# Mixing tiles moved between output products and routing steps, and a split moved from GpSimd to the Vector engine, in a fused attention, gMLP and mixture-of-experts kernel

## The chip, the cores and the metric

The kernel runs on one core of a Trainium2 chip. The core has a Tensor engine (PE, matrix products, with a separate queue for loading weights), a Vector engine (DVE), a Scalar engine (ACT), GpSimd (POOL), and SyncE (SP), which issues most of the DMAs. Each takes its instructions in order and waits for the others by semaphores. The metric is the device time of one execution in microseconds, as a median of several runs.

## What is computed

Three layers follow each other on two batches of 768 tokens with 384 features (8 heads of 48).

```
# 1 linear attention, per batch and head
state = alpha[t] * state + outer(k[t], v[t]);  y[t] = q[t] @ state
# 2 gMLP: d_ff = 1024, u and v have 512 columns each
h = gelu(x @ w_in);  u, v = split(h)
v_n = (v - mean(v)) / sqrt(var(v) + 1e-6) * g_ln
v_s = w_sg @ v_n + b_sg            # mixes the 768 tokens
x = x + (u * v_s) @ w_out
# 3 eight experts, one per token
fresh = argmax(x @ w_gate)         # e = fresh, or the token before's e when its local gate is >= 0.5
p = softmax(x @ w_gate)
out = p[e] * (relu(x @ w1[e]) @ w2[e])
```

## The kernel before, in words

**Products in three passes.** A float32 operand is split into a high part (`hi`, by ACT, L161) and a low part (`lo`, the difference, L162, by DVE or GpSimd as `pick` says), and `mm3` (L378) multiplies hi by hi, hi by lo and lo by hi. So one "term" is three products on PE.

**Stages.** Attention fills the first half. Then the second part of the gMLP and the routing run for each batch in two parts of tokens: 384 and 384 in batch 0, 512 and 256 in batch 1. From about 257 us to the end the eight experts run.

**The order of the middle** is a tuple, `SEQ`, which is worked through entry by entry. An entry has a letter, a batch and a part:

- `s`: `gmlp_s`, one mixing tile of 128 of the 512 columns. Eighteen products into `pvs`, then on DVE the bias and gain (L494), the factor u (L496), and the split into `g` (L161 on ACT, L162 on DVE). A part has four such tiles.
- `o`: `gmlp_out`, 36 products `po` from the four `g` and `w_out`, then three additions `x += po` on DVE (L512).
- `r`: one step of `route`. The first step multiplies x with the gate weights and the identity (`pr`, L527), takes logits (L530) and the maximum, and on DVE makes a chain of small operations (L545 to L559) that ends in `kf`. The second step turns `kf` round on PE (`pkr`, `pfr`, L564) and scans along the tokens (`er`, L571). The third counts the tokens of each expert (`pe`: L588, L589, L595, L597; `rsel` L600, `cl` L603). The fourth makes one-hot tiles `L` and `R` (L615, L616), multiplies them (`pid`, L618) and adds them to the slot table `tab` (L623). A further `r` of a finished part does nothing.
- `h1`: a step of batch 1's hidden layer. `l1`, `w0`, `k1`: loading the weights of expert 0, splitting them (`we_e_lo`), and loading two weights of expert 1.
- `e0`: `early` (L625). It reads the first slots of `tab` (`egid`), starts two gathers of token rows with GpSimd (`xs_first`, L726), and then calls `banks(5)`: the pool of eight PSUM banks is closed, and one of five, with three banks `px` beside it, is opened. Tiles that are written later in the program lie in the new pool.

The last part's route (batch 1, part 1) has more: its 256 rows are split into `xe` (L162, by the engine that `XEE` names), multiplied into `px` with the first rows (`px` L650 from `xs_first`, L661 from `xe`), and split to `xhl_e`, the first expert's input. Then the expert products begin (`ph_e` into `hhl_e` L756 and L757, then `pmy_e`).

**Who sets the order on an engine.** The program is written in SEQ's order. A tile scheduler then sets each engine's instruction order, looking a short way ahead, so that products of one step stand between those of another. Across the change of the PSUM pool it does not.

Of the kernel before, what the change touches and what calls it, by code (L numbers as in the profile page):

```python
# [38 lines left out]

HSEQ0 = 'vvuvuuvvuuuvuu'  # L40
HSEQ1 = 'vvvuvvvuuuuuuu'
SEQ = ('s00', 's00', 's00', 's00', 'x1', 's01', 's01', 's01', 'o00', 'r00', 's01', 'h1', 'r00', 'h1', 'r00', 'o01', 'h1', 'r00', 'r01', 'r00', 'h1', 'h1', 'r01', 'h1', 'r01', 'h1', 'h1', 'r01', 'h1', 'h1', 'h1', 'h1', 'r01', 'h1', 'h1', 's10', 's10', 's10', 's10', 'l1', 'w0', 's11', 'o10', 'w0', 's11', 'r10', 'r10', 's11', 'r10', 's11', 'r10', 'k1', 'k1', 'o11', 'r10', 'e0', 'r11', 'r11', 'r11', 'r11', 'r11')
INIT = ('u', 'u', 'u', 'w0', 'u', 'u', 'u', 'w1', 'w2')
ULOAD = (2, 3, 4, 5, 6, 7, 8, 7, 9, 9)
WIN = (4, 7, 6, 10, 13, 13)
# [18 lines left out]
SG = (3,) * 16  # L64
XS_E = (1,) * 12
NS_E = (1,) * 12
XEE = 0
NUNIT = 21

KEEP_T = -1.5 * 2.0 ** -23  # L70
# [2 lines left out]
class Layer:  # L73
# [441 lines left out]
    def route(self, b, hf, xT):  # L515
# [7 lines left out]
        for i in range(T):  # L523
# [11 lines left out]
            if end:  # L535
                xe = rw.tile([P, 2, DM], F32R, tag="xe", name=f"xe_{i}", bufs=T)
                self.split(xe[:, 0], xe[:, 1], xt, self.pick(XEE >> i))
                parts.append(xe)
# [288 lines left out]
    def run(self):  # L827
# [12 lines left out]
        with ExitStack() as c1:  # L840
# [84 lines left out]
            def step(nm):  # L925
                c, b, hf = nm[0], int(nm[1]), int(nm[2:3] or 0)
                if c == "s":
                    gs[b, hf].append(self.gmlp_s(b, hf, len(gs[b, hf]), vh[b], uh[b]))
                elif c == "o":
                    self.gmlp_out(b, hf, xT[b], gs[b, hf])  # L930
                    routes[b, hf] = self.route(b, hf, xT[b])
                elif c == "r":
                    next(routes[b, hf], None)
                elif c == "x":
                    xhl.append(self.x_split(1, xT[1]))
                    nonlocal_hidden.append(self.gmlp_h(1, xhl[1], vh[1], uh[1], HSEQ1))
                elif c == "h":
                    next(nonlocal_hidden[0])
                elif c == "e":
                    self.early()  # L940
                elif c == "k":
                    ahead.extend(self.expert_load(1, "e1", which=(len(ahead),)))
                elif c == "l":
                    raw.extend(self.expert_load(0, "e0"))
                elif c == "w":
                    ws[0].append(self.expert_split(raw.pop(0)))

            nonlocal_hidden, ahead = [], []
            for nm in SEQ:
                step(nm)  # L950
# [77 lines left out]
```

## Time and profile before

| what | us |
|---|---|
| median of 3 timed runs | 410.6 (410.39 to 410.85) |
| device time of the profiled execution | 409.02 |
| its span | 407.3 |
| PE busy | 380.8 (94% of the span) |
| DVE busy | 304.0 (75%) |
| ACT busy | 201.9 (50%) |
| POOL busy | 94.0 (23%) |

The profiled execution is one run, 1.6 us below the median of the timed ones, and has 1.7 us outside of its span. In the page, "busy" is time with an instruction of the engine under way, and a row of the timeline begins with the start in us from the span's start, then the time of the row, engine, line and operation, the output and inputs, the count, and in brackets the idle time before it and what ended it. Products on PE overlap in their rows: the distance of two starts is what one costs.

### The profile page before, as it was taken

How to read it: one execution, taken by the hardware profiler on the slowest of the kernel's cores; microseconds unless marked ns; L12 is line 12 of the kernel's file. 1: busy time of each engine (PE TensorE's matmuls, PEld its weight loads, DVE VectorE, ACT ScalarE, POOL GpSimd, SP SyncE). 2: the span in 40 equal slices, each digit the busy share in tenths (PEclk: the TensorE clock that was granted, in tenths of full speed). 3: DMA queues.
4: the chain of work that ended last, by engine and by line, in shares of the span. 5: the costliest groups of instructions: out<-in, count | busy, mean ns of one | idle time of the engine just before them, and what ended most of it. 6: DMA issues, size and time to landing. Idle time of an engine off the chain costs nothing. (4 is left out here: it accounts for less than half of the span.)

```text
span 407.3 us, 7658 instructions
## 1 busy us (share of the span) xinstructions
PE 380.8 (94%) x2798; PEld 328.1 (81%) x2798; DVE 304.0 (75%) x721; ACT 201.9 (50%) x465; POOL 94.0 (23%) x114
## 2 busy tenths in 40 slices
PE   8995997999999997999999896999899999999992
PEld 3663555678777996898988794899899999999991
DVE  7999999274777799866967876979886685994220
ACT  2534545465594644436562422758475563943110
POOL 1533753332240321000000004515222141300101
PEclk9997998599999999999999999999999999999998
DMA  8988877001123210110150263999756749200000
GB/s 219 300 214 209 228 217 211 22 23 36 59 53 110 92 39 2 59 38 23 33 202 2 77 228 89 362 310 354 268 174 224 259 135 330 65 0 33 32 2 26
DMA packets 34743, 54.56 MB, mean 134 GB/s; under 512 B 6243, under 2 KB 24957, under 8 KB 34704
## 3 DMA queue, kind: packets, MB, share of 16 engines
q1 hardware_dynamic: 32528, 48.08, 37.8%
q0 software_dynamic: 2176, 5.98, 4.7%
q8 instruction: 23, 0.38, 0.4%
q14 instruction: 16, 0.13, 0.1%
HBM read 46.91 MB, written 5.55 MB: 129 GB/s over the span
## 5 line engine op out<-in xcount | busy, mean ns | idle before, releaser
L378 PE MATMUL ph_e<-xhl_e,we_e_hi 128*128 128x256 f32 x384 | 69.2, 282 | 0.1
L162 DVE TENSOR_TENSOR we_e_lo<-wr_e,we_e_hi 128x384 fp32r<-128x384 f32 (+1 forms) x112 | 61.5, 608 | 9.3 <-ACT we_e_hi L161 4.8
L378 PE MATMUL pmy_e<-we_e_hi,hhl_e 128*128 128x384 f32 x256 | 67.0, 338 | 1.6 <-DVE hhl_e L757 1.6
L161 ACT ACTIVATE we_e_hi<-wr_e 128x384 fp32r<-128x384 f32 (+1 forms) x112 | 55.2, 564 | 26.6 <-PE pmy_e L378 17.8
L378 PEld LDWEIGHTS ph_e<-xhl_e,we_e_hi 128*128 128x128 f32 x384 | 59.4, 188 | 0.6 <-DVE xhl_e L162 0.6
L378 PE MATMUL ph_e<-xhl_e,we_e_lo 128*128 128x256 f32 x192 | 53.8, 281 | 0.0
L378 PEld LDWEIGHTS pmy_e<-we_e_hi,hhl_e 128*128 128x128 f32 x256 | 46.3, 188 | 1.8 <-DVE hhl_e L757 1.8
L378 PE MATMUL pmy_e<-we_e_lo,hhl_e 128*128 128x384 f32 x128 | 42.8, 336 | 0.0
L771 POOL DMA_INDIRECT out_dram<-my_e,sid x16 | 16.5, 1032 | 101.1 <-DVE my_e L770 87.5
L756 ACT ACTIVATE hhl_e<-ph_e 128x256 fp32r<-128x256 f32 x64 | 23.1, 382 | 32.7 <-PE ph_e L378 32.2
L232 POOL TENSOR_SCALAR_AFFINE_SELECT at<-at 128x384 f32<-128x384 f32 x32 | 29.1, 931 | 38.8 <-ACT at L230 38.7
L378 PEld LDWEIGHTS ph_e<-xhl_e,we_e_lo 128*128 128x128 f32 x192 | 36.7, 191 | 0.0
L757 DVE SCALAR_TENSOR_TENSOR hhl_e<-ph_e,hhl_e 128x256 fp32r<-128x256 f32 x64 | 24.2, 416 | 12.1 <-ACT hhl_e L756 12.1
L378 PE MATMUL pvs<-sg_lo,v_hi 128*128 128x384 f32 (+2 forms) x96 | 32.3, 337 | 0.0
L378 PE MATMUL pvs<-sg_hi,v_hi 128*128 128x384 f32 (+2 forms) x96 | 32.2, 340 | 0.0
L378 PE MATMUL pvs<-sg_hi,v_lo 128*128 128x384 f32 (+2 forms) x96 | 31.3, 336 | 0.0
L378 PE MATMUL pv<-wv_hi,xhl 128*128 128x512 f32 x72 | 26.6, 430 | 0.0
L378 PE MATMUL pu<-xhl,wu_hi 128*128 128x384 f32 x96 | 25.6, 344 | 0.0
L378 PE MATMUL po<-g,wo_hi 128*128 128x384 f32 (+2 forms) x96 | 25.0, 342 | 0.1
L378 PEld LDWEIGHTS pmy_e<-we_e_lo,hhl_e 128*128 128x128 f32 x128 | 24.1, 188 | 0.0
L770 DVE TENSOR_SCALAR my_e<-pmy_e,xs_e 128x384 f32<-128x384 f32 x16 | 9.8, 615 | 18.5 <-PE pmy_e L378 18.4
L280 PE MATMUL py<-at,io 128*64 128x128 f32 (+1 forms) x192 | 21.0, 294 | 2.0 <-ACT at L230 2.0
(196 smaller groups left out, 793.9 us busy)
## 6 DMA issues: line engine op xcount, KB each, us to landing
wr_e<-in_moe_w_dram SPq DMA_DIRECT2D x32, 768.0 KB, 7.3
io<-in_alpha_dram SPq DMA_DIRECT2D x16, 169.8 KB, 5.5
io<-in_k_dram SPq DMA_DIRECT2D x16, 168.0 KB, 5.6
io<-in_q_dram SPq DMA_DIRECT2D x16, 168.0 KB, 5.1
io<-in_v_dram SPq DMA_DIRECT2D x16, 144.0 KB, 4.7
sraw<-in_moe_w_sg_dram SPq DMA_DIRECT2D x3, 768.0 KB, 4.7
x2d<-xt SPq DMA_DIRECT2D x12, 192.0 KB, 2.0
x<-y SPq DMA_DIRECT2D x24, 72.0 KB, 2.5
```

The source lines that it names most:

```text
L161: return (self.nc.scalar.activation(out=hi, in_=src, func=AF.Copy), eng.tensor_tensor(out=lo, in0=src, in1=hi.bitcast(F32), op=ALU.subtract))
L162: eng.tensor_tensor(out=lo, in0=src, in1=hi.bitcast(F32), op=ALU.subtract))
L232: nc.gpsimd.affine_select(out=at[:, j], in_=at[:, j], compare_op=ALU.is_ge, fill=0.0, base=0, pattern=[[0, NCH], [1, P]], channel_multipli ...
L280: nc.tensor.matmul(py[64 * j:64 * j + m, cs], g["v"][:, o:o + m], at[:, j, c, :], start=True, stop=not inter)
L378: self.nc.tensor.matmul(out, l[a], r[c], start=start and i == 0 and p == 0, stop=stop and i == n - 1 and p == 2)
L756: nc.scalar.activation(out=hh, in_=ph, func=AF.Relu)
L757: nc.vector.scalar_tensor_tensor(out=hl, in0=ph, scalar=0.0, in1=hh.bitcast(F32), op0=ALU.max, op1=ALU.subtract)
L770: nc.vector.tensor_scalar(out=y, in0=py, scalar1=prob[i], scalar2=None, op0=ALU.mult)
L771: nc.gpsimd.indirect_dma_start(out=self.out2, out_offset=bass.IndirectOffsetOnAxis(ap=sid[:, i:i + 1], axis=0), in_=y, in_offset=None, bou ...
```

## The change

Two constants change. In SEQ, batch 0 has one mixing tile of part 1 between `o00` and the first `r00` instead of ahead of `o00`. In batch 1, `o10` comes ahead of all four tiles of part 1, and the tiles stand between its routing steps; the fifth, empty, `r10` goes; and `e0` now stands ahead of `k1`, `k1` and `o11`. `XEE` goes from 0 to 3: for the last two tiles of 128 rows the low part `xe` is made by DVE and not by GpSimd.

```diff
-SEQ = (... 'x1', 's01', 's01', 's01', 'o00', 'r00', 's01', 'h1', ...
-       's10', 's10', 's10', 's10', 'l1', 'w0', 's11', 'o10', 'w0', 's11', 'r10', 'r10', 's11', 'r10', 's11', 'r10',
-       'k1', 'k1', 'o11', 'r10', 'e0', 'r11', ...)
+SEQ = (... 'x1', 's01', 's01', 'o00', 's01', 'r00', 's01', 'h1', ...
+       's10', 's10', 's10', 's10', 'l1', 'w0', 'o10', 'w0', 's11', 'r10', 's11', 'r10', 's11', 'r10', 's11', 'r10',
+       'e0', 'k1', 'k1', 'o11', 'r11', ...)
-XEE = 0
+XEE = 3
```

What it does to the instruction order is shown at three places of batch 1. In these rows the first number of a name is the batch; of `pvs` and `vs` the second is the tile of columns and the third the part, of `po` the second is the row block and the third the part, of `pe`, `pr` and `kf` the second is the part.

On PE, at the first part's output products, before:

```order
L378 MATMUL pvs_1_0_1_2507<-sg2_hi_1552,v1_3_hi_2145 128x256
L378 MATMUL pvs_1_0_1_2507<-sg2_lo_1553,v1_3_hi_2145 128x256
L378 MATMUL pvs_1_0_1_2507<-sg2_hi_1552,v1_3_lo_2146 128x256
L378 MATMUL po_1_0_0_2532<-g_1_0_0_2410,wo_hi_1562 128x512
L378 MATMUL po_1_1_0_2533<-g_1_0_0_2410,wo_hi_1562 128x512
L378 MATMUL po_1_2_0_2534<-g_1_0_0_2410,wo_hi_1562 128x512
L378 MATMUL pvs_1_1_1_2582<-sg0_hi_1378,v1_0_hi_1909 128x256
L378 MATMUL pvs_1_1_1_2582<-sg0_lo_1379,v1_0_hi_1909 128x256
```

The same place after:

```order
L378 MATMUL pvs_1_0_0_2391<-sg2_hi_1552,v1_3_lo_2146 128x512
L378 MATMUL pvs_1_1_0_2416<-sg2_hi_1552,v1_3_lo_2146 128x512
L378 MATMUL pvs_1_2_0_2441<-sg2_hi_1552,v1_3_lo_2146 128x512
L378 MATMUL pvs_1_3_0_2466<-sg2_lo_1553,v1_3_hi_2145 128x512
L378 MATMUL pvs_1_3_0_2466<-sg2_hi_1552,v1_3_lo_2146 128x512
L378 MATMUL po_1_0_0_2507<-g_1_0_0_2410,wo_hi_1562 128x512
L378 MATMUL po_1_1_0_2508<-g_1_0_0_2410,wo_hi_1562 128x512
L378 MATMUL po_1_2_0_2509<-g_1_0_0_2410,wo_hi_1562 128x512
L378 MATMUL pvs_1_0_1_2557<-sg0_hi_1378,v1_0_hi_1909 128x256
```

The first tile of part 1 (`pvs_1_0_1`), whose products stood ahead of the first `po`, now follows the first three of them, and the end of the first tile of part 0 (`pvs_1_0_0`) stands five products ahead of `po`. The second tile of part 1 (`pvs_1_1_1`) goes from there to the middle of the twelve `pr`, 15 of its products behind the first four and three behind the last.

On DVE, in the chain from the logits of batch 1's first part to `kf`, before:

```order
L547 TENSOR_SCALAR kf_1_0_2639<-lg_1_0_2606 128x4
L552 TENSOR_TENSOR d_1_0_2647<-lg_1_0_2606,m_1_0_2641 128x32
L549 MEMSET nk_1_0_2640 1x1
L550 MEMSET kf_1_0_2639 1x1
L555 TENSOR_TENSOR ik_1_0_2649<-iotam_1239,nk_1_0_2640 128x32
L557 SCALAR_TENSOR_TENSOR ca_1_0_2651<-d_1_0_2647,ik_1_0_2649 128x32
L559 TENSOR_REDUCE kf_1_0_2639<-ca_1_0_2651 128x4
```

The same chain after:

```order
L547 TENSOR_SCALAR kf_1_0_2615<-lg_1_0_2582 128x4
L494 SCALAR_TENSOR_TENSOR vs_1_1_1_2649<-pvs_1_1_1_2630,gln_1253,bsg_1256 128x256
L552 TENSOR_TENSOR d_1_0_2623<-lg_1_0_2582,m_1_0_2617 128x32
L549 MEMSET nk_1_0_2616 1x1
L550 MEMSET kf_1_0_2615 1x1
L496 TENSOR_TENSOR vs_1_1_1_2649<-vs_1_1_1_2649,u_1_0_2129 128x256
L555 TENSOR_TENSOR ik_1_0_2625<-iotam_1239,nk_1_0_2616 128x32
L578 TENSOR_REDUCE sm_1_0_2670<-ex_1_0_2668 128x4
L557 SCALAR_TENSOR_TENSOR ca_1_0_2627<-d_1_0_2623,ik_1_0_2625 128x32
L579 TENSOR_SCALAR sm_1_0_2670<-sm_1_0_2670 128x4
L559 TENSOR_REDUCE kf_1_0_2615<-ca_1_0_2627 128x4
```

The two DVE operations of the tile that moved (L494 and L496 of `vs_1_1_1`) and two small softmax sums now stand inside of the chain.

On PE, from the counting of batch 1's first part to its slot table, before:

```order
L597 MATMUL pe_1_0_2701<-oh_1_0_2707,onesb_1229 128x8
L378 MATMUL po_1_0_1_2766<-g_1_1_0_2526,wo_hi_1562 128x256
L378 MATMUL po_1_0_1_2766<-g_1_1_0_2526,wo_lo_1563 128x256
...
L378 MATMUL po_1_2_1_2768<-g_1_1_2_2695,wo_hi_1562 128x256
L618 LDWEIGHTS L_1_0_2721
L618 MATMUL pe_1_0_2701<-R_1_0_2722,L_1_0_2721 128x96
L378 MATMUL po_1_0_1_2766<-g_1_1_2_2695,wo_hi_1562 128x256
```

The same place after:

```order
L597 MATMUL pe_1_0_2701<-oh_1_0_2707,onesb_1229 128x8
L618 LDWEIGHTS L_1_0_2721
L618 MATMUL pe_1_0_2701<-R_1_0_2722,L_1_0_2721 128x96
...
L378 MATMUL po_1_0_1_2791<-g_1_1_0_2576,wo_hi_1562 128x256 x2
L378 MATMUL po_1_0_1_2791<-g_1_1_0_2576,wo_lo_1563 128x256
```

Before, most of the second part's 36 `po` products stood between the counting (L597) and the four products of `pid` (L618). Now the four follow the counting at once, and all 36 `po` come behind them. In the last part's route, the six `px` products of the second gather (L650), which stood behind L588 and L589, now stand ahead of them. On DVE the two `xe` operations now stand right behind `kf` L559 and behind the scan L571; GpSimd has two instructions fewer.

## Rows read from the trace of the kernel before

**Rows 1.** The page's part 1: busy time, share, instructions.

```profile
PE 380.8 (94%) x2798; PEld 328.1 (81%) x2798; DVE 304.0 (75%) x721; ACT 201.9 (50%) x465; POOL 94.0 (23%) x114
```

**Rows 2.** The view of PE's waits: us in total, times, longest.

```profile
PE pfr L564 <- DVE kf L559: 3.2, 3, 2.7
PE pmy_e L378 <- DVE hhl_e L757: 1.6, 1, 1.6
```

**Rows 3.** Windows: length; PE, PEld, DVE, ACT, POOL busy; granted clock, DMA share, GB/s.

```profile
30.00:34.00 4.00, 1.11 (x16) 0.51 (x12) 4.00 (x11) 0.45 (x1) 0.00 (x0) 1.00 0.79 166
34.00:42.00 8.00, 6.53 (x46) 4.02 (x46) 7.90 (x14) 4.76 (x14) 3.46 (x4) 0.57 0.78 227
150.00:156.00 6.00, 5.89 (x31) 4.92 (x30) 6.00 (x12) 3.56 (x8) 1.84 (x2) 1.00 0.00 0
248.00:252.00 4.00, 1.33 (x9) 0.79 (x9) 3.74 (x9) 1.32 (x5) 2.77 (x3) 1.00 0.70 199
```

**Rows 4.** PE's timeline at the end of batch 0's output products.

```profile
158.51 0.97 PE L527 MATMUL pr<-rt,x 128*128 128x137 f32 x6 [2.44 <-DVE x L512]
```

**Rows 5.** PE's timeline, batch 1, from the last mixing products to the scan.

```profile
213.73 0.28 PE L378 MATMUL pvs<-sg_hi,v_hi 128*128 128x256 f32 x1
...
218.46 0.28 PE L378 MATMUL pvs<-sg_hi,v_hi 128*128 128x256 f32 x1
...
219.53 0.86 PE L378 MATMUL po<-g,wo_hi 128*128 128x512 f32 x3
...
229.94 3.07 PE L527 MATMUL pr<-rt,x 128*128 128x137 f32 x24
...
234.81 0.39 PE L564 MATMUL pfr<-identb,kf 128*1 128x128 bf16 x4 [0.26 <-DVE kf L559]
```

**Rows 6.** DVE's timeline, batch 1, at the mixing tiles.

```profile
215.94 0.75 DVE L494 SCALAR_TENSOR_TENSOR vs<-pvs,gln,bsg 128x512 f32<-128x512 f32 x1 [2.23 <-PE pvs L378]
216.72 0.69 DVE L496 TENSOR_TENSOR vs<-vs,u 128x512 f32<-128x512 f32 x1
...
225.41 0.42 DVE L496 TENSOR_TENSOR vs<-vs,u 128x256 f32<-128x256 f32 x1
```

**Rows 7.** ACT's timeline, the first high part of batch 1.

```profile
217.45 0.63 ACT L161 ACTIVATE g<-vs 128x512 fp32r<-128x512 f32 x1 [4.33 <-DVE vs L496]
```

**Rows 8.** PE's timeline from the counting of batch 1's first part on.

```profile
240.04 0.28 PE L378 MATMUL pvs<-sg_hi,v_lo 128*128 128x256 f32 x1
240.16 0.40 PE L378 MATMUL po<-g,wo_hi 128*128 128x256 f32 x2
...
245.84 1.68 PE L527 MATMUL pr<-rt,x 128*128 128x137 f32 x12 [0.73 <-DVE tab L623]
```

**Rows 9.** DVE's timeline over the same stretch.

```profile
240.37 0.48 DVE L494 SCALAR_TENSOR_TENSOR vs<-pvs,gln,bsg 128x256 f32<-128x256 f32 x1 [0.85 <-PE pvs L378]
240.97 0.19 DVE L600 TENSOR_TENSOR rsel<-pe,oh 128x32 f32<-128x32 f32 x1
...
244.04 0.30 DVE L616 TENSOR_SCALAR R<-iotac,cl,tok 128x96 f16<-128x96 f16 x1
244.54 1.09 DVE L512 TENSOR_TENSOR x<-po,x 128x256 f32<-128x256 f32 x3 [0.20 <-PE po L378]
```

**Rows 10.** PE's timeline, the last part's route up to the experts.

```profile
251.53 1.46 PE L650 MATMUL px<-ew,xs_first 128*128 128x256 f32 x6
252.92 0.20 PE L588 MATMUL pe<-onesb,er 1*128 1x1 bf16 x2
...
257.45 0.84 PE L378 MATMUL ph_e<-xhl_e,we_e_hi 128*128 128x256 f32 x2
```

**Rows 11.** DVE's timeline, the last part's chain to `kf`.

```profile
248.29 2.55 DVE L557 SCALAR_TENSOR_TENSOR ca<-d,ik 128x16 f32<-128x16 f32 x1
```

**Rows 12.** GpSimd's timeline at the same time.

```profile
248.86 1.94 POOL L162 TENSOR_TENSOR xe<-xt,xe 128x384 fp32r<-128x384 f32 x2
```

**Rows 13.** DVE's timeline ahead of the first expert's second product.

```profile
284.40 1.95 DVE L162 TENSOR_TENSOR we_e_lo<-wr_e,we_e_hi 128x384 fp32r<-128x384 f32 x4
```

More of the change, by code (lines that the diff above doesn't have):

```diff
@@ L41 @@
 HSEQ1 = 'vvvuvvvuuuuuuu'
-SEQ = ('s00', 's00', 's00', 's00', 'x1', 's01', 's01', 's01', 'o00', 'r00', 's01', 'h1', 'r00', 'h1', 'r00', 'o01', 'h1', 'r00', 'r01', 'r00', 'h1', 'h1', 'r01', 'h1', 'r01', 'h1', 'h1', 'r01', 'h1', 'h1', 'h1', 'h1', 'r01', 'h1', 'h1', 's10', 's10', 's10', 's10', 'l1', 'w0', 's11', 'o10', 'w0', 's11', 'r10', 'r10', 's11', 'r10', 's11', 'r10', 'k1', 'k1', 'o11', 'r10', 'e0', 'r11', 'r11', 'r11', 'r11', 'r11')
+SEQ = ('s00', 's00', 's00', 's00', 'x1', 's01', 's01', 'o00', 's01', 'r00', 's01', 'h1', 'r00', 'h1', 'r00', 'o01', 'h1', 'r00', 'r01', 'r00', 'h1', 'h1', 'r01', 'h1', 'r01', 'h1', 'h1', 'r01', 'h1', 'h1', 'h1', 'h1', 'r01', 'h1', 'h1', 's10', 's10', 's10', 's10', 'l1', 'w0', 'o10', 'w0', 's11', 'r10', 's11', 'r10', 's11', 'r10', 's11', 'r10', 'e0', 'k1', 'k1', 'o11', 'r11', 'r11', 'r11', 'r11', 'r11')
 INIT = ('u', 'u', 'u', 'w0', 'u', 'u', 'u', 'w1', 'w2')
```

## The prediction

> **What bounds the kernel now.** I read the page's part 1 first. PE is busy 94% of the span, the others 75% and less [rows 1]: PE sets the time, and an edit changes it only where it fills or opens an idle stretch on PE. So the next view is PE's waits. Of those that the change can touch, the two large ones are the wait of `pfr` for `kf`, 2.7 of its 3.2 us in one place, and of the first expert's second product for `hhl_e`, 1.6 [rows 2]; the third is the wait of batch 0's `pr` for x, 2.44 [rows 4]. Between them PE's rows follow each other. From 257.45 on [rows 10] it is the experts' turn; with PE that full, what arrives there later ends later by as much. So the sum is the shift of that start, less what the wait for `hhl_e` gives back. It is made on the profiled execution (409.02 us, span 407.3). That run lies 1.6 below the median of 410.6, and I add the sum to the median.
>
> **Batch 0's tile.** The same 18 products are done before `pr`, only behind the first three `po` instead of ahead. `pr` waits for L512, and DVE, which is busy for 6.00 of 6 us ahead of that [rows 3], does its operations up to L512 in the same order. I take 0. From above, 0.4, if a reordered pair there lengthens DVE's row; nothing in it can start L512 sooner, so no gain.
>
> **Batch 1: the start of the output products.** A 256-column product costs 0.12 us (240.04 to 240.16 [rows 8]). Before, nine of the first part-1 tile went from 213.73 to 214.81, then 16 wide ones to 218.46, that is 0.228 each, and nine more to 219.53, where `po` began without a wait [rows 5]. After, the 16 run from 213.73 and end at 217.38. Their result isn't ready for `po` by then. The first tile's last product is the fifth from the end: done at 217.38 - 4 x 0.228 = 216.47. Before, it was done at 214.81 + 4 x 0.228 = 215.72 and L494 began at 215.94, 0.22 later, so now at 216.69. The second tile's L494 now precedes the first's L496; starts in that pair are 0.78 apart [rows 6], so L496 starts at about 218.2 and ends at 218.9, ACT's high part (0.63 [rows 7]) at about 219.5. PE idles **2.1 us** there. From that point the 36 `po` and 18 products of a part-1 tile take as long as the 36 and 18 of before, 10.41 us [rows 5]: `pr` starts as early as before, with one tile (18 x 0.12 = 2.16) still undone.
>
> **The chain to `kf`.** 15 of these 18 products stand inside of `pr`: its end moves by 15 x 0.12 = 1.8. Behind that, DVE's chain has two operations more, 0.48 [rows 9] and 0.42 [rows 6]. `pfr` therefore moves by 1.8, if both fall into time that DVE waits anyway, up to 2.7. I take **2.4**, as the operations stand inside of the chain but its logits had DVE work ahead of them before, which is over sooner than `pr` now. From `pfr` to the counting the work is unchanged: 2.4 arrives there whole.
>
> **The slot table of the first part.** This is the largest term. Before, PE started `po` of the second part at 240.16 [rows 8]; they covered DVE's work from `rsel` at 240.97 to the last `R`, which ends at 244.34 [rows 9], and `pr` began at 245.84 after a wait of 0.73 [rows 8]. After, all `po` stand behind the last `pid`. So PE has some 0.3 us of small products between 240.16 and 244.34 (in before's clock), then `pid` to about 244.55, then 36 x 0.12 = 4.3 us of `po` to 248.9. Before, L512 began 0.2 after its last `po`, and three took 1.09 [rows 9]; the third now ends about 0.7 after the last `po`, at 249.6, and the last third of `pr` (1.68 in all [rows 8]) behind it at 250.2, against 245.84 + 1.68 = 247.5 before. That is **+2.7**; bounds +2.4 (the last addition overlaps more) and +3.3 (no overlap of L512 with `pr`).
>
> Here a page bears on the clock. Rows first: the granted clock stayed at 1.00 (the upper level, 2.4 GHz) over a stretch of 4 us with 1.33 us of PE work, and averaged 0.57 over the 8 us that follow a stretch of 4 us with 1.11 us of work [rows 3]; at full use of the lower level (1.2 GHz) it would be 0.5. The new stretch, about 0.5 us of work in 4.2, is emptier than either. The Trainium skill, "TensorE: Matmul & The Clock Gate", section "Why this matters for your kernels", asks to leave no long idle gap between bursts of matmuls, since the clock then falls to the lower level. This trace agrees once and once not. By it the sum would have the clock rival's price, below.
>
> **The last part's route.** `ca` takes 2.55 us where an operation as small takes 0.19 (`rsel`) [rows 9], and ends at 250.84, when GpSimd's two `xe` subtractions end (248.86 + 1.94 = 250.80 [rows 11, 12]). PE waits 2.7 for the `kf` behind it [rows 2]. With `xe` on DVE, GpSimd has nothing there that could hold `ca`; I take `ca` at 0.2, a gain of 2.35. The Trainium skill, "SBUF — State Buffer", section "Who interferes with whom", has it that a DVE instruction with two SBUF inputs and a GpSimd instruction that reads SBUF lock each other out, which the row agrees with; without such a cause `ca` would stay, and the sum would be 2.35 higher. Against the gain: one `xe` (0.49 on DVE, by the rows of the same size [rows 13]) stands ahead of the scan, where PE is at the twelve `px` products of 2 x 1.39 us (251.53 to 252.92 is six [rows 10]) and so doesn't feel it. These twelve were done ahead of L595 before, too, six on either side of L588; now L588 comes behind all, and DVE's turn between L588 and L595 (`oh`) no longer lies under the last six. I take 0.35 for it, two small operations' time. Net **-2.0**; bounds -1.6 (0.4 for `xe` after all) and -2.6 (the turn costs nothing, and a part of the idle time behind L595 goes).
>
> **The expert stage.** Of the wait for `hhl_e` (1.6), DVE's four `we_e_lo` ahead of it (1.95, so 0.49 each [rows 13]) are the cause; two of them now stand behind it: **-0.95**. Bounds 0, if DVE is late for another reason, and -1.6.
>
> **Sum.** 0 + 2.4 + 2.7 - 2.0 - 0.95 = +2.15; 410.6 + 2.15 = **412.8 us**. With every bound: 1.8 + 2.4 - 2.6 - 1.6 = 0.0 and 0.4 + 2.7 + 3.3 - 1.6 + 0 = +4.8, so 410.6 to 415.4 for this case. Measurement can tell about 0.2% (0.8 us) from no change.
>
> **Rivals.** *The clock falls* after the empty stretch. For: the rows of 30 to 42 us. Against: 248 to 252 with the clock at 1.00, where PE had idled 2.7 us in one piece [rows 2, 3], while the small products of L597 and `pid` break the new stretch up. Price: 8 us at 0.57 are 8 x 0.43 = 3.4 us of PE work lost [rows 3]; 412.8 + 3.4 = 416.2.
>
> *No change*: all bounds on the low side, 410.6. For: each is a row's own number. Against: they would have to come together.
>
> *Faster*: the tile inside of `pr` covers the chain to `kf` as a filler should. In the sum its work moves `pr` and with it the chain; if the wait for `kf` is what gives way, `pfr` moves only by the 2.1 idle less the 1.4 that PE waited between `pr` and `pfr` (233.0 to 234.81, less 0.4 of `pkr`) [rows 5], +0.7, not 2.4. With -2.6 in the tail, -1.6 at `hhl_e`, and +2.4: -1.1, 409.5 us. It decides from the point where the two moved DVE operations are done while PE still multiplies; then `pfr` comes less than 1.8 later. Against it: three of the tile's products stand behind the last `pr`, so its L494 can't have started when the logits are complete.
>
> **Chances.** Forecast 0.50, clock 0.22, no change 0.10, faster 0.18. Of the forecast's and the clock's cases nearly all are slower by over 0.2%; a part of the forecast's low side counts as same: slower 0.68, same 0.13, faster 0.19. The range takes in the clock case and most of the faster one: 409.0 to 416.8.
>
> **What would show it.** Before the first `po` of batch 1, an idle time of about 2 us that ends with ACT's high part. `pfr` of the first part 2.4 later relative to the last wide `pvs`. Between L597 and the first `po` of the second part, some 4 us with four `pid` products and the idle time charged to L616. In the last part `ca` at about 0.2 us, and a `pfr` wait below 0.6. The wait for `hhl_e` below 1. The clock in the 10 us behind the empty stretch: 1.00, or about 0.5 to 0.6. The prediction is wrong if PE fills the stretch between L597 and `po`, if `ca` stays long, or if the experts start as early as before.

## The result, and the profile after

The changed kernel takes **414.49 us** (median of 5, 413.33 to 415.83) where the kernel before takes 410.6 (409.14 to 411.77 beside it): a ratio of 1.0116, interval 1.0087 to 1.0146. It is slower, by 3.9 us at the medians. The forecast was 412.8, on the slower side and within its range, but with little more than half of the loss.

The profiled execution of the changed kernel took 413.33, with a span of 411.6. I begin where [rows 1] began, at the busy times.

```profile
PE 381.2 (93%) x2798; PEld 329.4 (80%) x2798; DVE 302.1 (73%) x723; ACT 202.0 (49%) x465; POOL 92.6 (23%) x112
```

PE has as many instructions as before and 0.4 us more of busy time, in a span that is 4.3 longer: its idle time rises from 26.5 to 30.4 us. So waits are the first thing to read, and the clock the second, since a busy PE need not be PE at its full clock. PE's waits answer to [rows 2]; the columns are the waiting line, what it waits for, and the total, count and longest in us.

```profile
PE pe L618 <- DVE R L616: 3.0, 3, 2.3
PE pr L527 <- DVE x L512: 2.9, 2, 2.3
PE po L378 <- ACT g L161: 2.7, 2, 1.9
...
PE pfr L564 <- DVE kf L559: 1.1, 3, 0.5
PE pkr L564 <- DVE kf L550: 0.8, 1, 0.8
...
PE ph_e L378 <- DVE gid L678: 0.5, 1, 0.5
PE pxt_e L740 <- DMA xs_e<-x2d,gid: 0.3, 1, 0.3
```

The 2.7 us wait of the last `pfr` has gone, and so has the wait for `hhl_e`, which has no row any more. In their place stand a wait of `pid` (L618) for `R`, one of the first `po` for ACT's high part, a second wait of a `pr` for x (its row has 2.9 in 2 where before it had one of 2.44 [rows 4]), and small ones at the start of the experts. To put prices on them I cut the program at milestones on PE that both kernels have, and took the starts of those rows from PE's timeline:

- **batch 0's route**: from its first six `pr` to its next twelve `pr`;
- **head**: from L595 of batch 0's second part to `pfr` of batch 1's first part;
- **slot table**: from there to the first `pr` of batch 1's second part;
- **last route**: from there to `pxt_e` (L740), with which the second expert's input begins;
- **experts**: from there to the output's last transfer.

| us, one profile each | before | after | difference |
|---|---|---|---|
| start of batch 0's `pr` | 158.51 | 157.55 | -0.96 |
| batch 0's route | 3.59 | 5.15 | +1.56 |
| up to L595 | 29.6 | 29.6 | 0 |
| head | 43.12 | 45.85 | +2.73 |
| slot table | 11.03 | 15.14 | +4.11 |
| last route | 21.05 | 19.06 | -1.99 |
| experts | 133.77 | 132.44 | -1.33 |
| end | 400.66 | 404.78 | +4.12 |

The first row is nothing of the change: in two more profiles of the kernel before the same `pr` starts at 157.06 and 157.20, since the granted clock of 60 to 90 us averages 0.83 in both and 0.77 in the first one. The other rows are read one by one.

**The head.** PE's timeline, which answers to [rows 5]: start, duration, instruction, and in brackets the idle time ahead of it.

```profile
219.99 0.96 PE L378 MATMUL po<-g,wo_hi 128*128 128x512 f32 x3 [1.86 <-ACT g L161]
...
231.22 1.20 PE L527 MATMUL pr<-rt,x 128*128 128x137 f32 x8 [0.61 <-DVE x L512]
...
237.27 0.38 PE L564 MATMUL pkr<-identb,kf 128*1 128x128 bf16 x4 [0.82 <-DVE kf L550]
238.14 0.38 PE L564 MATMUL pfr<-identb,kf 128*1 128x128 bf16 x4 [0.49 <-DVE kf L559]
```

PE waits 1.86 us ahead of the first `po` and 0.61 ahead of `pr`; before, both began without a wait. Then it waits 0.82 at `pkr` and 0.49 at `pfr`, 1.31 together. That is no more than before, where the `pfr` of [rows 5] waited 0.26 and the `pkr` ahead of it 1.15:

```profile
234.16 0.38 PE L564 MATMUL pkr<-identb,kf 128*1 128x128 bf16 x4 [1.15 <-DVE kf L550]
```

So the 2.73 fall into two pieces. From L595 to `pr` it is 0.68 more (38.93 instead of 38.25), nearly all of it the new wait of 0.61: DVE now does three `we_e_lo` (1.90) ahead of the additions L512, the first of which starts at 230.48 instead of 229.20. From `pr` to `pfr` it is 2.05 more (6.92 instead of 4.87), of which 1.80 lie inside `pr`, among whose products the moved tile's now stand.

**The slot table.** PE's timeline over the stretch of [rows 8]:

```profile
243.52 0.24 PE L597 MATMUL pe<-oh,onesb 128*128 128x32 bf16 x4
246.07 0.22 PE L618 MATMUL pe<-R,L 128*128 128x96 f16 x1 [2.31 <-DVE R L616]
246.78 0.20 PE L618 MATMUL pe<-R,L 128*128 128x96 f16 x1 [0.49 <-DVE R L616]
247.16 0.62 PE L618 MATMUL pe<-R,L 128*128 128x96 f16 x2 [0.17 <-DVE R L616]
247.56 0.78 PE L378 MATMUL po<-g,wo_hi 128*128 128x256 f32 x2
...
248.35 0.63 PE L378 MATMUL po<-g,wo_hi 128*128 128x256 f32 x2
248.78 0.41 PE L378 MATMUL po<-g,wo_lo 128*128 128x256 f32 x1
...
250.77 0.40 PE L378 MATMUL po<-g,wo_hi 128*128 128x256 f32 x2
251.01 0.28 PE L378 MATMUL po<-g,wo_lo 128*128 128x256 f32 x1
...
253.28 1.63 PE L527 MATMUL pr<-rt,x 128*128 128x137 f32 x12
```

Between L597 and `po`, 4 us pass with four small products in them. Then two `po` take from 248.35 to 248.78, 0.215 each; later, from 250.77 to 251.01, two take 0.24, that is 0.12 each. The windows (length; PE, PEld, DVE, ACT, POOL busy; granted clock, DMA share, GB/s) say why:

```profile
158.00:162.00 4.00, 4.00 (x17) 4.00 (x16) 3.38 (x7) 0.49 (x1) 0.00 (x0) 0.57 0.00 0
...
244.00:247.50 3.50, 0.66 (x3) 0.39 (x4) 3.48 (x18) 0.59 (x2) 0.10 (x1) 0.96 0.98 372
247.50:250.40 2.90, 2.87 (x14) 2.87 (x14) 0.42 (x2) 0.00 (x0) 1.54 (x2) 0.50 0.21 78
250.40:253.00 2.60, 2.60 (x23) 2.60 (x22) 0.24 (x1) 0.00 (x0) 0.71 (x1) 0.96 0.60 154
```

Behind the stretch in which PE has 0.66 us of work in 3.5, the granted clock is 0.50, that is 1.2 GHz, for 2.9 us in which PE is busy for 2.87. The first line shows the same at batch 0: 0.57 behind the 2.25 us in which `pr` waits for x.

**The last route and the experts.** Rows of DVE and PE that answer to [rows 11, 10 and 13]:

```profile
255.68 0.17 DVE L557 SCALAR_TENSOR_TENSOR ca<-d,ik 128x16 f32<-128x16 f32 x1
...
256.12 0.27 PE L564 MATMUL pfr<-identb,kf 128*1 128x128 bf16 x2 [0.30 <-DVE kf L559]
256.55 2.75 PE L650 MATMUL px<-ew,xs_first 128*128 128x256 f32 x12
...
288.72 1.01 DVE L162 TENSOR_TENSOR we_e_lo<-wr_e,we_e_hi 128x384 fp32r<-128x384 f32 x2
289.65 0.41 DVE L757 SCALAR_TENSOR_TENSOR hhl_e<-ph_e,hhl_e 128x256 fp32r<-128x256 f32 x1
289.99 1.01 DVE L162 TENSOR_TENSOR we_e_lo<-wr_e,we_e_hi 128x384 fp32r<-128x384 f32 x2
```

`ca` takes 0.17 instead of 2.55, `pfr` waits 0.30 instead of 2.67, and all twelve `px` follow in one row. In the expert stage DVE's `we_e_lo` come two and two with an `hhl_e` between, no longer four in a row.

### The profile page after: what moved, and what is told of

It reads as the page before. It is cut to its first block, busy times and chain, and to the rows that moved or that the text cites. A ratio compares the mean times of both kernels' runs of the same rounds, so it can differ in the third digit from the quotient of the medians.

```text
span 411.6 us, 7661 instructions
## 1 busy us (share of the span) xinstructions
PE 381.2 (93%) x2798; PEld 329.4 (80%) x2798; DVE 302.1 (73%) x723; ACT 202.0 (49%) x465; POOL 92.6 (23%) x112
## 5 line engine op out<-in xcount | busy, mean ns | idle before, releaser
L232 POOL TENSOR_SCALAR_AFFINE_SELECT at<-at 128x384 f32<-128x384 f32 x32 | 29.6, 944 | 39.9 <-ACT at L230 39.9
L378 PE MATMUL po<-g,wo_hi 128*128 128x384 f32 (+2 forms) x96 | 25.9, 354 | 2.7 <-ACT g L161 2.7
L378 PE MATMUL pv<-wv_hi,xhl 128*128 128x512 f32 x72 | 25.7, 417 | 0.0
L726 POOL DMA_INDIRECT xs_e<-x2d,gid x16 | 18.7, 1171 | 17.8 <-DVE gid L678 12.5
```

Source lines behind the costliest of these rows:

```text
L232: nc.gpsimd.affine_select(out=at[:, j], in_=at[:, j], compare_op=ALU.is_ge, fill=0.0, base=0, pattern=[[0, NCH], [1, P]], channel_multipli ...
L378: self.nc.tensor.matmul(out, l[a], r[c], start=start and i == 0 and p == 0, stop=stop and i == n - 1 and p == 2)
L726: self.gather = nc.gpsimd.indirect_dma_start(out=xs, out_offset=None, in_=self.x2d[:n], in_offset=bass.IndirectOffsetOnAxis(ap=gid[:, i:i ...
```

## The experiments

Each kernel was timed against the kernel before on the same chip. For the first four the latter's median was 410.23 (408.02 to 414.39), for the next four 409.63 (407.58 to 413.84); the last three are one profile each. The segments of all the profiles stand in a table behind the experiments.

### The last rows' low parts alone (a1)

```diff
 # kernel before
-XEE = 0
+XEE = 3
```

> The kernel before with XEE = 3 alone. My theory: GpSimd's subtractions held the small DVE operation ca; without them ca takes about 0.2 us instead of 2.55, the wait of pfr for kf in the last part falls from 2.7 us to about 0.3, and the experts start about 2 us sooner: 2.0 to 2.4 us faster, ratio 0.994 to 0.995. Rival: ca was long for another reason, or the wait moves on to the scan or to sel: ratio 1.000.

Measured: 406.94 (405.68 to 407.24), ratio 0.9906, 0.9872 to 0.9940. Faster, and by more than expected. But the last route is only 0.22 shorter, 20.83 instead of 21.05. DVE and PE in it:

```profile
248.46 0.56 DVE L162 TENSOR_TENSOR xe<-xt,xe 128x384 fp32r<-128x384 f32 x1
248.94 0.17 DVE L557 SCALAR_TENSOR_TENSOR ca<-d,ik 128x16 f32<-128x16 f32 x1
...
249.36 0.27 PE L564 MATMUL pfr<-identb,kf 128*1 128x128 bf16 x2 [0.66 <-DVE kf L559]
...
250.22 1.56 PE L650 MATMUL px<-ew,xs_first 128*128 128x256 f32 x6 [0.26 <-DMA xs_first<-x2d,egid]
252.45 1.56 PE L650 MATMUL px<-ew,xs_first 128*128 128x256 f32 x6 [0.67 <-DMA xs_first<-x2d,egid]
```

`ca` is as short as the forecast had it, and `pfr` waits 2.0 less. But then `px` waits for the gathered rows, `xs_first`, first 0.26 and then 0.67. The long wait for `kf` had covered the gathers' landing. Most of the rest goes into the step from the second six `px` to the next product, L661: 3.36 instead of 2.48, since the counting (L588, L595) comes behind all twelve here and no longer under the last six. What PE won at one semaphore it gave back in the steps behind it. The other 1.86 of this profile's gain lies in the experts, where the wait for `hhl_e` is gone.

### The gathers' start put back (a2)

```diff
 # changed kernel
-... 'e0', 'k1', 'k1', 'o11', 'r11', ...
+... 'k1', 'k1', 'o11', 'e0', 'r11', ...
```

> The changed kernel with e0 put back behind k1, k1 and o11. My theory: the second part's po stand between the counting and pid again, so the empty stretch and the low clock behind it go (4.1 us in the profile), while the later pfr (+2.7) and the shorter last route (-2.0) stay, and 0 to -1.3 at the first expert's wait: 410.0 to 411.3 us, near the kernel before. Rival: the stretch at the slot table is not what costs, since later waits would have absorbed it: 413 us or more.

Measured: 412.89 (411.06 to 414.77), ratio 1.0056, 1.0027 to 1.0086. Better than the changed kernel's 1.0116, but worse than expected. The slot table takes 10.20 instead of 15.14, so `e0`'s place alone opened the empty stretch: with `e0` back, `po` stands behind L597 again. The last route, however, is 22.88, longer than the changed kernel's 19.06 and than before's: `px` waits 1.40 for `xs_first`, behind a wait of 0.67 for `pfr`, and the clock falls behind these waits. The row of `px`, then the window that it lies in:

```profile
253.16 4.46 PE L650 MATMUL px<-ew,xs_first 128*128 128x256 f32 x12 [1.40 <-DMA xs_first<-x2d,egid]
...
253.20:257.50 4.30, 4.30 (x12) 3.31 (x12) 0.00 (x0) 0.00 (x0) 0.00 (x0) 0.62 0.82 229
```

The twelve `px` take 4.46 here, at a granted clock of 0.62, and 2.75 in the changed kernel. These 1.7 are the clock; without them the last route would be about as long as before's 21.05.

### The gathers' start moved alone (a3)

```diff
 # kernel before
-... 'k1', 'k1', 'o11', 'r10', 'e0', 'r11', ...
+... 'e0', 'k1', 'k1', 'o11', 'r11', ...
```

> The kernel before with e0 alone moved ahead of k1, k1 and o11 (and the empty r10 left out); XEE stays 0, the mixing tiles stay. My theory: the empty stretch between L597 and po appears by itself, +2.8 us, and the clock falls behind it for some 3 us, +1.3: 413.4 to 414.9 us. Rival: the stretch costs nothing by itself, as the tail's wait for GpSimd absorbs it: 410.6 to 411.5.

Measured: 411.83 (410.19 to 412.67), ratio 1.0029, 0.9999 to 1.0058: less than expected. The slot table takes 16.67, the clock falls as it did in the changed kernel, and the last route is 19.05, the changed kernel's to 0.01. Yet in this kernel GpSimd still makes `xe`. The window behind the empty stretch, then GpSimd and DVE in the last route:

```profile
244.90:248.00 3.10, 3.10 (x14) 3.10 (x15) 0.11 (x1) 0.00 (x0) 2.24 (x2) 0.50 0.22 60
...
245.30 1.24 POOL L726 DMA_INDIRECT xs_first<-x2d,egid  x1 [4.07 <-DMA wr_e<-in_moe_w_dram]
...
254.62 1.95 POOL L162 TENSOR_TENSOR xe<-xt,xe 128x384 fp32r<-128x384 f32 x2 [6.78 <-ACT xe L161]
...
253.95 0.17 DVE L557 SCALAR_TENSOR_TENSOR ca<-d,ik 128x16 f32<-128x16 f32 x1
...
254.88 0.77 DVE L579 TENSOR_SCALAR sm<-sm 128x2 f32<-128x2 f32 x1
```

`ca` takes 0.17 all the same. GpSimd's `xe` waits for ACT and starts at 254.62, when `ca` has been over for half a microsecond; beside it `sm` (L579) takes 0.77, which nobody on PE waits for. The difference is small: `ca` begins 0.67 ahead of `xe` here, and in the kernel before, where it was held until `xe` ended, 0.57 ahead [rows 11, 12]. And the gathers start at 245.30, 8 us ahead of this chain, so that `xs_first` lies ready when `px` comes. Both things come from `e0`'s place, none from `XEE`.

### The empty stretch filled (a4)

```diff
 # changed kernel, in route() behind L610
         if end:
             self.late(cl[:, 0], parts)
+        elif b == B - 1:
+            self.fill(9, last)
```

This adds nine products of 128x512, whose result nobody reads, behind L597 of batch 1's first part. Later lines move by two.

> The changed kernel with nine products of 128x512 on a constant (some 2 us of work whose result nobody reads) behind L597, in the empty stretch ahead of pid. My theory: PE stays busy there, the granted clock stays at 1.00 over the 36 po behind it, and these take 4.3 us instead of 5.7: 1.3 us faster than the changed kernel, about 413.2. Rival: the low clock there is chance of that one profile, and the fill gives nothing or delays pid: 414.5 or more.

Measured: 411.46 (410.15 to 413.42), ratio 1.0037, 1.0011 to 1.0064, where the changed kernel has 1.0116: a larger gain than expected. The same windows as in the changed kernel:

```profile
244.00:247.50 3.50, 2.32 (x18) 1.92 (x17) 2.33 (x12) 0.00 (x0) 0.55 (x1) 1.00 0.72 272
247.50:250.40 2.90, 2.90 (x27) 2.90 (x25) 0.54 (x2) 0.00 (x0) 1.70 (x2) 1.00 0.29 85
```

The clock stays at 1.00 and PE does 27 products in the 2.9 us in which it did 14. The fill delays nothing: the first `pid` starts 2.54 behind L597, and in the changed kernel 2.55. The slot table takes 13.82: that is what the order itself costs, 2.79 above before, and the rest of the 4.11, 1.32 in that profile, was the clock. The timed runs agree with the profile: the mean granted clock of a run has a median of 0.971 over these twelve and of 0.960 over the changed kernel's five. (This profile's batch 0 kept its clock too, of which more below.)

### Batch 0's tile alone (b1)

```diff
 # kernel before
-SEQ = (... 's01', 's01', 's01', 'o00', 'r00', ...
+SEQ = (... 's01', 's01', 'o00', 's01', 'r00', ...
```

> The kernel before with batch 0's tile alone moved behind o00. My theory: pr still waits for L512, which DVE's full queue sets, so nothing changes: 409.8 to 410.8 us against 410.2. The clock behind that wait falls in some runs with or without the tile. Rival: the tile makes the low clock behind the wait more frequent, 411 to 411.8.

Measured: 408.92 (406.71 to 411.76), ratio 0.9979, 0.9950 to 1.0009: no difference that can be told, though the median lies below the expected range. What it shows of the last route is worth more. DVE, GpSimd and PE there:

```profile
247.73 2.59 DVE L579 TENSOR_SCALAR sm<-sm 128x2 f32<-128x2 f32 x1
...
248.33 1.95 POOL L162 TENSOR_TENSOR xe<-xt,xe 128x384 fp32r<-128x384 f32 x2
...
249.96 1.56 PE L650 MATMUL px<-ew,xs_first 128*128 128x256 f32 x6 [1.72 <-DMA xs_first<-x2d,egid]
```

In this profile `pr` no longer waits 0.73 for `tab`, the slot table is 0.83 shorter (10.20) and the chain runs about half a microsecond earlier against GpSimd: `ca` begins 1.12 ahead of `xe` instead of 0.57. Now `sm` is the operation that takes as long as `xe`, 2.59, and `ca` escapes. `pfr` waits 0.33 instead of 2.67, but the last route is only 0.11 shorter (20.94), since `px` waits 1.72 for `xs_first`. So the wait of [rows 2] that the forecast took away with `XEE` can go without `XEE`, and even with the shorter slot table the two segments gain only 0.94 together, not the 2.35 of the forecast.

### Batch 1's tiles alone (b2)

```diff
 # kernel before
-... 'l1', 'w0', 's11', 'o10', 'w0', 's11', 'r10', 'r10', 's11', 'r10', 's11', 'r10', ...
+... 'l1', 'w0', 'o10', 'w0', 's11', 'r10', 's11', 'r10', 's11', 'r10', 's11', 'r10', ...
```

> The kernel before with batch 1's four mixing tiles alone moved behind o10 and between its routing steps; e0 and XEE as before. My theory: PE idles 1.9 us ahead of the first po and pfr comes 2.7 later, as in the changed kernel, and nothing behind gives it back: 412.7 to 413.2. Rival: the last part's wait for GpSimd (2.7 us before) takes it up: 410.5 to 411.

Measured: 409.78 (408.24 to 411.88), ratio 1.0011, 0.9984 to 1.0038. No loss that can be told, and less than the 2.5 us or more that were expected. Its head takes 45.83, so the 2.7 us are lost there all the same, with the same 1.86 ahead of `po`; 2.4 of them come back later: the slot table 10.54 (-0.5) and the experts 131.92 (-1.9, no wait for `hhl_e`). Its last route, 22.92, is 0.8 shorter than in the two profiles of the kernel before that also lost the clock there (below).

### The changed kernel with GpSimd's `xe` (b3)

```diff
 # changed kernel
-XEE = 3
+XEE = 0
```

> The changed kernel with XEE back at 0 (xe on GpSimd). By the prediction's term, ca is held by GpSimd again: 2.4 us slower than the changed kernel, 416.9. Rival theory, from the run with e0 alone moved: with e0 ahead of k1 and o11, xe comes only behind ca on GpSimd, so ca takes 0.2 us either way, and XEE gives nothing in the changed kernel: 414.0 to 415.0.

Measured: 413.51 (412.44 to 416.19), ratio 1.0091, 1.0049 to 1.0132: not slower than the changed kernel. The last route is 19.06, as with `XEE` at 3. The forecast's term for `XEE` isn't there in this program; GpSimd's `xe` starts at 258.80, 0.3 behind the end of the chain, and `ca` takes 0.18. The profile itself (416.19) is longer since the clock fell in three places: at batch 0, behind the wait ahead of `po` (head 47.36) and behind the empty stretch (16.21).

### The low parts, and batch 0's wait filled (c1)

```diff
 # kernel before with XEE = 3; mm3 keeps its last product
+        self.fill(8 * ((b, hf) == (0, 0)), self.last)   # gmlp_out, behind the L512 additions
```

Eight products of 128x512, again read by nobody, behind batch 0's first output products.

> The kernel before with XEE = 3 and with eight products of 128x512 on a constant (some 2 us whose result nobody reads) behind batch 0's last po, where PE waits 2.4 us for L512. My theory: in most runs the clock falls to its lower level behind that wait for some 3.5 us, which costs 1.6; with PE busy there it stays at 1.00: 405.0 to 405.8 us, against 406.9 with XEE = 3 alone. Rival: the clock there does not depend on that wait, or the fill delays pr: 406.9 or more.

Measured: 405.98 (405.43 to 407.34), ratio 0.9917, 0.9887 to 0.9947. That can't be told from a1's 0.9906, so whether the fill pays stays open. PE ahead of batch 0's `pr`, and the window behind:

```profile
154.80 1.46 PE L107 MATMUL warm<-busy 128*128 128x512 bf16 x6
156.93 0.97 PE L527 MATMUL pr<-rt,x 128*128 128x137 f32 x6 [0.67 <-DVE x L512]
...
158.00:162.00 4.00, 4.00 (x29) 4.00 (x28) 3.27 (x9) 0.86 (x2) 0.00 (x0) 1.00 0.00 0
```

The wait shrinks from 2.44 to 0.67 without `pr` starting later, and the clock is 1.00 in this profile. But it is 1.00 in six profiles without a fill, too, and the mean granted clock of c1's nine runs (median 0.968) is no higher than that of a1's seven (0.969).

### Both kernels once more (d1, d2, d3)

The kernel before twice and the changed kernel once, unchanged, for the clock.

> The kernel before, unchanged, for a second profile. My theory: its times scatter because the clock falls in some runs behind the 2.4 us wait of batch 0's pr (low for about 3.5 us, +1.6) and in some behind the waits of the last part's route (+2 to 3). A run of 408 to 409.2 has neither, one of 410 to 411 has one, one above 412 has both. Rival: the clock is at 1.00 in both places and the scatter comes from the attention stage.

> The kernel before, unchanged, for a third profile: as with the second, the time and the places of the low clock go together by theory, +1.6 for the one and +2 to 3 for the other.

> The changed kernel, unchanged, for a second profile. My theory: the clock falls behind the empty stretch at the slot table in every run, for 3 us or more (+1.3 to +2.9), as in the three profiles so far in which e0 stands ahead of k1 and nothing fills the stretch; batch 0's wait may or may not add 1.6. 413 to 416 us. Rival: the low clock at the slot table is chance, and this profile has 1.00 there and a time near 412.

Measured: 410.64, 410.35 and 412.58. The kernel before, profiled again (PE's wait, then two windows, of the first of them):

```profile
249.71 0.27 PE L564 MATMUL pfr<-identb,kf 128*1 128x128 bf16 x2 [2.67 <-DVE kf L559]
...
248.00:251.00 3.00, 1.29 (x7) 1.08 (x8) 2.74 (x7) 0.00 (x0) 1.40 (x2) 0.97 0.60 183
251.00:254.00 3.00, 3.00 (x10) 2.03 (x10) 0.26 (x2) 0.00 (x0) 0.00 (x0) 0.50 0.40 78
254.00:258.00 4.00, 4.00 (x17) 2.56 (x17) 1.92 (x10) 0.18 (x1) 0.00 (x0) 0.54 1.02 387
```

The wait is the one of [rows 2], 2.67. But where the forecast's profile kept 1.00 behind it [rows 3], both of these have 0.50 and then 0.54 and 0.53, and their last route takes 23.75 and 23.74 instead of 21.05. The same wait in the same program gave either outcome, and the low one costs 2.7 us. Yet both runs are only 1.6 and 1.3 us longer than the forecast's profile (409.02), since batch 0's `pr` starts 1.3 to 1.5 earlier in them: a part of the scatter does lie in the attention stage, as the rival had it. In d3 the clock falls at batch 0 and behind the empty stretch (slot table 14.96), as in the first profile of the changed kernel; its time, 412.58, lies a little below the expected range.

### All profiles by segment

| us | batch 0's route | head | slot table | last route | experts | end |
|---|---|---|---|---|---|---|
| before | 3.59 | 43.12 | 11.03 | 21.05 | 133.77 | 400.66 |
| before (d1) | 3.61 | 43.12 | 11.03 | 23.75 | 133.80 | 402.00 |
| before (d2) | 3.58 | 43.12 | 11.02 | 23.74 | 133.56 | 401.82 |
| after | 5.15 | 45.85 | 15.14 | 19.06 | 132.44 | 404.78 |
| after (d3) | 5.17 | 45.85 | 14.96 | 19.13 | 132.60 | 403.89 |
| a1 | 5.16 | 43.11 | 11.03 | 20.83 | 131.91 | 398.85 |
| a2 | 5.18 | 45.85 | 10.20 | 22.88 | 133.00 | 403.55 |
| a3 | 5.15 | 43.12 | 16.67 | 19.05 | 133.08 | 403.68 |
| a4 | 3.60 | 45.82 | 13.82 | 19.28 | 132.15 | 401.81 |
| b1 | 3.57 | 43.11 | 10.20 | 20.94 | 133.70 | 399.13 |
| b2 | 3.60 | 45.83 | 10.54 | 22.92 | 131.92 | 402.55 |
| b3 | 5.16 | 47.36 | 16.21 | 19.06 | 132.47 | 407.26 |
| c1 | 3.60 | 43.12 | 11.02 | 20.71 | 132.10 | 397.08 |

Read it by columns. The head is 43.12 or 45.85, by the place of batch 1's tiles and nothing else, but for b3 with its clock. The slot table is long where `e0` stands early. The last route is 19.1 to 19.3 where `e0` stands early, whatever `XEE` says. Batch 0's route is 3.6 or 5.2 whether its tile was moved (after, a2, a4, b1, b3) or not.

## Why the prediction was right, and where it was not

**Direction and sum of the order.** Right. With the filled stretch's 13.82, the changed order gives 2.73 + 2.79 - 1.99 - 1.33 = +2.20 in these profiles; the forecast's sum was +2.15. The filled kernel's own profile, in which the clock holds from batch 0 on as it did in the forecast's, gives 2.70 + 2.79 - 1.77 - 1.62 = +2.10. The sum came out partly by terms that were right and partly by one that was right in size for the wrong reason.

**Batch 0's tile: 0.** Right for the time: b1 can't be told from no change. The 1.56 that the profile after loses there is the clock, and it came with the tile moved and with it unmoved (a1, a3), behind idle times of the same length.

**The head: +2.4.** Right, measured +2.73, at the upper bound of 2.7. The mechanism is in the main the one described: PE idles 1.86 (forecast 2.1) ahead of `po`, since ACT's high part of the first tile comes late, and the products inside `pr` lengthen it by 1.80 (forecast 1.8). Two smaller steps were off. "`pr` starts as early as before" put at nothing what measured 0.68, mostly a wait for L512, which now stands behind three `we_e_lo` on DVE; and the two more operations in DVE's chain, for which the forecast added 0.6, cost 0.25. The two nearly cancel. What the forecast didn't have is that this loss need not arrive: b2, with the tiles alone, can't be told from the kernel before.

**The slot table: +2.7.** Right for the order: 2.79, by the filled kernel. The 36 `po` no longer cover DVE's work from `rsel` to the last `R`. a2 and a3 show that `e0`'s place is the cause and not the tiles'. Which part of `e0` keeps `po` behind `pid`, the change of the PSUM pool or its other operations, no run separates; the pool is the likely one, as the tiles of `o11` lie in the new pool when `e0` stands ahead of it.

**The clock rival.** This is the first of two steps that failed. The likeliest case had the clock hold behind the empty stretch, because it had held at 248 to 252 in [rows 3], and because the small products break the stretch up. It fell in every one of the four profiles with the stretch left empty (after, d3, a3, b3), and not in the filled one. The row that had argued against it was one draw: in d1 and d2 the clock fell at that same place. The price was put at 3.4; the slot table shows 1.1 to 2.9 above 13.82 (the 2.9 is a3's, whose tiles stand as before). Filling the stretch took the ratio from 1.0116 to 1.0037. The Trainium skill, "TensorE: Matmul & The Clock Gate", section "Why this matters for your kernels", which the prediction set beside these rows, asks for no long idle gap between bursts of matmuls. In these four profiles the clock fell behind a stretch whose longest single idle time was 2.3 us, and in some executions it fell, in others not, behind the 2.25 us at batch 0 and the 2.67 us in the last route. Each of these is shorter than the gap that the page names, so the row that the prediction counted against the page does not contradict it, and the falls here go beyond what it states.

**The last route: -2.0.** The size is right (-1.99), the cause wrong, so that the agreement is luck. In the changed kernel `pfr` comes 2.42 sooner behind `pr` (forecast 2.35) and the way from the first `px` to L661 is 0.40 longer (forecast 0.35). But the step that failed is "with `xe` on DVE, GpSimd has nothing there that could hold `ca`; I take `ca` at 0.2, a gain of 2.35". `ca` did go to 0.17, and the gain from that is 0.2 (a1) and none in the changed kernel (b3). The wait for `kf` had hidden a second one, for `xs_first`. With the first gone, the second ends last: 0.93 in a1, 1.72 in b1, 1.40 in a2, 1.19 in b2. What brings the 2.0 is `e0`'s place: a3, which moves `e0` alone, has the same last route. The gathers start 4.7 us ahead of `pr` in the changed kernel and 6.3 in a3, where before they started 0.4 behind it, so that `px` finds its rows; and `ca` is short in a3 although GpSimd still makes `xe`. Why `ca` escapes there stays open: `xe` starts as long behind `pr` as before (3.07 in a3 and b3, 3.02 before). The prediction had noted that `e0` moves and had costed only what it takes away, not the earlier landing that it brings.

**The expert stage: -0.95.** Measured -1.33, inside the bounds. The wait went entirely, by DVE's order. But that order isn't the change's own: it is gone as well in a1, b2, b3 and c1, and is there at 1.3, 0.8 and 0.5 us in b1, a2 and a3. Edits that stand ahead of the experts change DVE's order there: `we_e_lo` come two and two in a1, a4, b2, b3 and c1, four in a row in a2, a3 and b1. So this gain can be had once, whichever part brings it. It is one reason why the parts don't add: their ratios alone are 0.9906 (`XEE`), 1.0029 (`e0`), 1.0011 and 0.9979 (tiles), and together 1.0116.

**The median.** The forecast added +2.15 to the median of before, as if that had the clock of the profiled run. By d1 and d2 the kernel before loses 2.7 in its last route in some executions, and 409.02 + 2.7 = 411.7 is about the top of the first five times; d1 and d2 themselves, with a shorter attention stage, took 410.64 and 410.35. The sums by rows reach the changed kernel's times: 409.02 + 2.20 + 1.1 = 412.3 with the clock lost behind the stretch alone, and 409.02 + 2.20 + 2.9 + 1.56 = 415.7 with the largest loss there and batch 0's, against 412.58 to 415.83 measured. How often each loss occurs the profiles are too few to say, so the split of the 3.9 between medians into order (2.2) and clock (the rest) is worked out, not measured. The runs' mean granted clocks point the same way (medians: 0.960 in the changed kernel, 0.971 in the filled one, 0.966 in the thirty runs of the kernel before beside it), but don't say in which stage. The same holds for a1: its rows explain 2.1 of a gain of 3.3, and that the rest is the last route's clock, kept because its one long wait has become three short ones (its times spread over 1.6 us where the kernel before spreads over 6.4), is argued and not shown by a run of its own; a1's median clock, 0.969, is higher than the 0.966 of the kernel before beside it.

**A better kernel.** `XEE` = 3 alone, the one part of the change that the changed kernel makes no use of, is faster than both: 406.94, ratio 0.9906.

## What to carry to other kernels

Before a wait is counted as a gain, find what PE would wait for next if it were gone: look at when the data of the next products lands, not at the semaphore that came last. When a step is moved early to start its transfers sooner, look at what else it carries that may keep other work from filling PE (here, probably, the change of the PSUM pool), and cost the two apart. And a granted clock read from one profile is one draw, so profile twice before a clock of 1.00 behind a wait of 2 to 3 us counts as evidence.

## What the runs showed of the hardware

The granted clock behind one and the same PE wait was not the same from execution to execution. Behind the 2.67 us in the last route of the kernel before it was 1.00 once and 0.50 twice; behind the 2.2 to 2.4 us ahead of batch 0's `pr` it averaged 0.57 to 0.69 from 158 to 162 us in six profiles (after, d3, a1, a2, a3, b3) and 1.00 in six; in the thirteenth, c1, the wait was filled. One such fall costs 1.1 to 2.9 us. Small products did not prevent it: the four `pid` in the empty stretch are 128x96 each.

Which small DVE operation is drawn out beside GpSimd's subtraction of two 128x384 tiles differs by tenths of a microsecond: `ca` (2.55) in the kernel before, `sm` (2.59 and 2.44) in b1 and b2, and in a3 `sm` for only 0.77, where it began 0.26 behind GpSimd's. In the first three the drawn-out one began 0.57, 0.60 and 0.45 ahead of GpSimd's and ended with it; `ca` in a3 and b3 began 0.67 ahead and was not drawn out (0.17 and 0.18). GpSimd came straight from a gather in the first three and had been idle for over 6 us in a3 and b3; whether that decides it no run shows. The Trainium skill, "SBUF — State Buffer", section "Who interferes with whom", which the prediction set beside `ca`, counts DVE operations with two SBUF inputs among those that contend with GpSimd's reads, and `tensor_scalar`, which `sm` is, in certain modes; that `ca` is held agrees, and whether `sm` ran in such a mode no row here shows.
